# Probabilities of pairs six to 31 copied by DMA into fp32r tiles and transposed as fp32r; second-layer sums in place; the 1e-9 added by GpSimd

## Chip, core and metric

The kernel runs on one core of one Trainium2 chip. The metric is the device time in microseconds (us). The core has five engines with an instruction queue each: PE (TensorE, matmuls; PEld is its weight load), DVE (VectorE), ACT (ScalarE), POOL (GpSimd) and SP (SyncE, which here only issues DMAs). SBUF is the memory that engines compute from, PSUM the one that PE writes to.

## What is computed

Attention with a decay for 8 batches of 8 heads, 576 tokens, head dimension 64, and behind it a token mix and a two-layer channel network, all in float32:

```python
scores = scale * np.matmul(q, k.transpose(0, 1, 3, 2))
cum = np.cumsum(np.log(np.clip(f, 0.0001, 1.0)), axis=-1)
scores = np.where(causal, -1e9, scores + cum[..., :, None] - cum[..., None, :])
attn = np.exp(scores - np.max(scores, axis=-1, keepdims=True))
attn = attn / (np.sum(attn, axis=-1, keepdims=True) + 1e-09)
x = np.matmul(attn, v)                       # heads side by side: (8, 576, 512)
u = x + (x.transpose(0, 2, 1) @ U @ V).transpose(0, 2, 1)
out = u + np.maximum(u @ w_ch1, 0.0) @ w_ch2 # 512 -> 2048 -> 512
```

## The kernel before

**Pairs and slots.** Two heads make a pair; there are 32, four to a batch. A step handles one pair in ten slots, and works on three pairs at once: slots 0 to 3 score pair p for its first head (`score(p, 0, i)`, i the block of 128 queries), slots 4 and 5 the 64 last queries of both heads (`score_tail`), slots 6 to 9 the second head. In the same slots PE transposes the probabilities of the pair before (`turn_p`, `turn_tail`, `turn_small`), multiplies them with the values (`values`), and turns and ranks the results of the pair before that (`turn_x`, `ranks`). Parts of the token mix and of the first channel layers of the batch before fill the slots (`mix_units`, `ffn_units`). When the pairs are through, at about 740 us, the other ten of 16 hidden blocks follow for all batches.

**Two kinds of pair.** Pairs 0 to 5 (`p < NF`) multiply in plain fp32. From pair six on, operands are split into a high and a low fp32r tile and multiplied in fp32r. The probabilities of all pairs are written as F32 by the exponential and transposed as F32 with `ident`; what comes out is split behind the transpose, by a copy on ACT (`PTh`) and a subtraction on DVE (`PTl`).

**One score's way.** PE writes scores into a bank of PSUM (`S`, two of them from pair six on). In the next slot DVE adds the mask and takes the extreme value (`top`, L387), ACT writes the exponential and its row sum (`use`, L395), and so frees the bank. `inverse` adds the two sums of the tail (POOL, L435), adds 1e-9 (DVE, L436) and inverts (DVE, L437).

**What sets the order.** `defer(phase, fn, slots)` puts work into a later slot, by phase. PE's order is written out by hand for all steps, SP's for step 0 and from step 8 on. ACT, DVE and POOL, and SP in steps 1 to 7, are ordered by a scheduler when the program is built. Each queue runs in its order: an instruction that waits holds up all behind it. A tile from a pool with n buffers waits until the tile n allocations earlier is read.

**Buffers near the change.** `P0` to `P3` have two buffers each, `Ptl` (tail probabilities) and `cr` (a half of a product) one, `ost` (a sum of the second layer on its way to DRAM) two.

Of the kernel before, what the change touches and what calls it, by code (L numbers as in the profile page):

```python
# [44 lines left out]
def tile_decay_attention_moe(ctx, tc, qk, v, f, U, V, w1, w2, out):  # L45
# [43 lines left out]
    sf2 = pool("sf2")  # L89
# [6 lines left out]
    sb3 = pool("sb3", 3)  # L96
    psF = ctx.enter_context(tc.tile_pool(name="psF", bufs=2, space=PSUM))
# [30 lines left out]
    ident = cst.tile([P, P], F32, name="ident")  # L128
    make_identity(nc, ident)
# [14 lines left out]
    def decay_log():  # L144
        fr = sb.tile([B * H, S], F32, tag="xT", name="fr")
        fl = sb.tile([B * H, S], F32, tag="cr", name="fl")
        cm = sb.tile([B * H, 4, S], F32R, tag="PT", name="cm")
        return fr, fl, cm
# [48 lines left out]

    def load_w(u):
# [4 lines left out]
        if kind == "w2":  # L203

            spare = xn[NX - 1].rearrange("p c d -> p (c d)").bitcast(I32)
            if fc % 2:
                raw, a = spare[:, 1536:2560], sb.tile([P, 512], I32, tag="w2a", name=f"stg{u}")
            else:
                raw, a = spare[:, 0:1024], spare[:, 1024:1536]
# [167 lines left out]

    def score(p, j, i):
# [25 lines left out]
    def score_tail(p, x):  # L404
# [14 lines left out]
        def use():  # L419
            if x == 1:  # L420
                z["ptl"] = sb.tile([P, S], F32, tag="Ptl", name=f"Ptl{p}")
                for y in range(2):
                    nc.scalar.activation(
                        z["ptl"][:, hw * y : hw * y + hw], z["tl"][y][:, :hw], AF.Exp, bias=z["nm"][:, 9:10],
                        scale=-1.0, accum_out=z["sm"][:, 8 + y : 9 + y],
                    )

# [3 lines left out]
    def inverse(p):  # L431
# [4 lines left out]
        nc.vector.tensor_scalar(sm[:, 0:9], sm[:, 0:9], 1e-9, None, op0=ALU.add)  # L436
# [12 lines left out]
    def turn_p(p, j, g):  # L449
# [16 lines left out]
        for x, (c, i) in enumerate(grp):  # L466
            nc.tensor.transpose(tp[:, P * x : P * x + P], z["P"][j][i][:, P * c : P * c + P], ident)  # L467
# [12 lines left out]
    def turn_tail(p):  # L480
        z = st[p]
        tp = z["tv"][:, 512:1024]
        for c in range(NM):
            nc.tensor.transpose(tp[:, P * c : P * c + P], z["ptl"][:, P * c : P * c + P], ident)
# [13 lines left out]
    def turn_small(pa, px):  # L498

        tq = psT.tile([P, 512], F32, tag="T", name=f"Ty{pa}_{px}")  # L500
        if pa is not None:
            nc.tensor.transpose(tq[0:64, 0:P], st[pa]["ptl"][:, MAIN:S], ident)
# [75 lines left out]
    def values(p, j):  # L578
# [4 lines left out]
        if j == 0:  # L583
            z["xT"] = sb.tile([P, S], F32, tag="xT", name=f"xT{p}")
            z["cr"] = sb.tile([P, S], F32, tag="cr", name=f"cr{p}")
        VS, xT, cr = z["VS"], z["xT"], z["cr"]
# [14 lines left out]
        def total():  # L601
            nc.vector.tensor_tensor(xT[OWN[j]], pv[OWN[j], X0 : X0 + S], cr[OTH[j]], op=ALU.add)
# [3 lines left out]
        defer(1, lambda: nc.scalar.copy(cr[OTH[j]], pv[OTH[j], X0 : X0 + S]))  # L606
# [66 lines left out]
    def mix_units(b):  # L673
# [38 lines left out]
        def tv():  # L712
# [9 lines left out]
            def use():  # L722
                for x, t in enumerate((uh, ul)):
                    if b < B - 1:
                        nc.sync.dma_start(ud[b, :, x], t.bitcast(F32)[:, :, 0:MAIN])
                    if b % 2:
                        jt = b // 2
                        nc.sync.dma_start(ud[B, :, x, :, P * jt : P * jt + P], t.bitcast(F32)[:, :, MAIN : MAIN + P])

            defer(4, use, 2)  # L730
# [5 lines left out]
    def ffn_units(b):  # L736
# [7 lines left out]
        for t0, nt in groups:  # L744
# [24 lines left out]
            def l2(x, part, t0=t0, g=g):  # L769
# [17 lines left out]
                def use():  # L787
                    if b == B - 1 and ci < NM:
                        nc.vector.tensor_tensor(X[:, ci], ps, X[:, ci], op=ALU.add)
                        return  # L790
                    ost = sf2.tile([P, DM], F32, tag="ost", name=f"ost{b}_{ci}")
                    if ci < NM:
                        nc.vector.tensor_tensor(ost, ps, X[:, ci], op=ALU.add)
                        nc.sync.dma_start(accd[b, ci], ost)
                    else:
                        nc.vector.tensor_tensor(ost[0:64], ps[0:64], X[0:64, NM], op=ALU.add)
                        nc.vector.tensor_tensor(ost[64:128], ps[64:128], xn[(b - 1) % NX][0:64, NM], op=ALU.add)
# [876 lines left out]
```

## Time and profile before

| what | value |
|---|---|
| median of three runs | 1217.29 us (1216.34 to 1217.51) |
| the profiled execution, its own time | 1216.95 us |
| its span, first to last instruction | 1215.1 us |
| granted TensorE clock, mean | 0.999 |
| busy share of the span | PE 98%, DVE 76%, ACT 64%, POOL 28% |
| busy from 94.9 to 642.2 us (25 steps) | PE 537.3, DVE 400.6, ACT 400.6, POOL 272.5 us of 547.3 |

How it is read: a line of groups names kernel line, engine, operation, output tile and input tiles, shape, how many, then busy us, mean ns of one, and idle time before them with what ended it. A timeline gives start and duration in us; instructions that follow one another are merged as x4, and their duration then runs from the first start to the last end. A matmul's duration holds its way through the array, which the next one overlaps, so the pace of PE is read from the distance of starts. "Pair 14" below is the one whose step begins at 269.8 us.

### The profile page before, as it was taken

To read this page: it belongs to the slowest core of one execution; us is meant where nothing else is said; L and a number is where in the kernel's file an instruction comes from. 1 tells how busy PE (TensorE), PEld (TensorE's weight loads), DVE (VectorE), ACT (ScalarE), POOL (GpSimd) and SP (SyncE) were. 2 spreads that over 40 slices of the span, in tenths; PEclk is the share of its full clock that TensorE was granted. 3 is DMA by queue.
4 is the path that set the end of the run, shared out by engine and by line. 5 is a ranking of instruction groups with operands and counts; after the bars stand their busy time and mean duration, and the time that the engine had idled before them with its cause. 6 is when DMAs were issued, how large, how long until landed. Compare 5 with 4: busy or idle time off the path is not lost.

```text
span 1215.1 us, 24243 instructions
## 1 busy us (share of the span) xinstructions
PE 1190.5 (98%) x8463; PEld 1101.9 (91%) x8463; DVE 917.9 (76%) x2302; ACT 779.0 (64%) x2045; POOL 335.9 (28%) x366
## 2 busy tenths in 40 slices
PE   8999999999999999999999999999999999999997
PEld 6888888998999988999988898888999999999997
DVE  8786778668777677767769899848868778687765
ACT  7787777767777667777667444335565565555553
POOL 3656654444545535555442100000000000000000
PEclk9999999999999999999999999999999999999999
DMA  6546235225244334335324566936765574654643
GB/s 201 154 135 177 63 90 179 77 80 169 70 109 150 89 95 136 98 82 166 101 69 143 186 213 235 332 134 225 255 216 184 170 235 149 233 194 154 200 114 105
DMA packets 111243, 187.38 MB, mean 154 GB/s; under 512 B 11241, under 2 KB 55529, under 8 KB 109073
## 3 DMA queue, kind: packets, MB, share of 16 engines
q1 hardware_dynamic: 110848, 185.57, 49.2%
q8 instruction: 67, 1.10, 0.4%
q14 instruction: 56, 0.45, 0.1%
q10 hardware_dynamic: 272, 0.26, 0.1%
HBM read 137.42 MB, written 48.37 MB: 153 GB/s over the span
## 4 chain that ended last, share of the span: by engine, by line
PE 84%; DVE 6%; ACT 5%; issue 1%; DMA 1%; POOL 1%; POOLq 0%; ACTq 0%; DVEq 0%
PE pf L1312 16%; PE B L779 11%; PE A L758 10%; PE po L1404 8%; PE V L591 4%; PE px L1404 4%; PE T L467 3%; PE S L366 3%; PE S L367 2%; PE Hb L1135 2%; PE O L1151 2%; PE pf L1404 2%; PE po L1419 2%; ACT G L320 2%; PE V L548 1%
## 5 line engine op out<-in xcount | busy, mean ns | idle before, releaser
L1535 ACT COPY mc<-pf 128x512 f32<-128x512 f32 x139 | 81.6, 587 | 169.0 <-PE pf L1312 169.0
L387 DVE CUSTOM_DVE_ANT_0 S<-S,mask 128x128 f32<-128x128 f32 (+3 forms) x256 | 125.2, 497 | 56.3 <-PE S L367 48.1
L395 ACT ACTIVATE P<-S,nm 128x128 f32<-128x128 f32 (+3 forms) x256 | 136.3, 534 | 44.6 <-DVE nm L387 43.7
L1463 POOL TENSOR_TENSOR xn<-xn,xn 128x512 f32<-128x512 f32 x1 | 1.3, 1267 | 530.0 <-DMA out_dram<-xn 530.0
L758 PE MATMUL A<-uh,w1h 128*128 128x256 f32 (+1 forms) x384 | 119.7, 312 | 0.0
L758 PE MATMUL A<-ul,w1h 128*128 128x256 f32 (+1 forms) x384 | 113.5, 295 | 0.0
L758 PE MATMUL A<-uh,w1l 128*128 128x256 f32 (+1 forms) x384 | 113.5, 295 | 0.0
L320 POOL CAST G<-qk 64x576 fp32r<-64x576 f32 x52 | 34.4, 661 | 243.1 <-PE St L367 155.2
L779 PE MATMUL B<-w2h,hh 128*128 128x512 f32 x216 | 88.4, 409 | 0.0
L467 PE MATMUL T<-ident,P 128*128 128x128 f32 x544 | 86.8, 275 | 0.0
L779 PE MATMUL B<-w2l,hh 128*128 128x512 f32 x216 | 85.1, 394 | 0.0
L779 PE MATMUL B<-w2h,hl 128*128 128x512 f32 x216 | 84.7, 392 | 0.0
L445 DVE TENSOR_TENSOR PT<-T,PT 128x512 fp32r<-128x512 f32 (+1 forms) x156 | 79.0, 530 | 6.5 <-ACT PT L442 4.7
L591 PE MATMUL V<-PT,VS 128*128 128x448 f32 (+2 forms) x416 | 79.5, 333 | 0.0
L336 POOL TENSOR_TENSOR G<-qk,G 64x576 fp32r<-64x576 f32 x52 | 74.5, 1433 | 7.3 <-ACT G L320 5.6
L442 ACT CAST PT<-T 128x512 fp32r<-128x512 f32 (+1 forms) x156 | 67.7, 466 | 13.8 <-PE T L467 11.7
L366 PE MATMUL S<-G 128*128 128x128 f32 x208 | 71.7, 348 | 4.8 <-ACT P L395 2.3
L335 POOL TENSOR_TENSOR G<-qk,G 64x576 fp32r<-64x576 f32 x52 | 74.6, 1434 | 3.8
L758 PEld LDWEIGHTS A<-uh,w1l 128*128 128x128 f32 x384 | 73.1, 190 | 0.3
L758 PEld LDWEIGHTS A<-uh,w1h 128*128 128x128 f32 x384 | 72.8, 190 | 0.4
L758 PEld LDWEIGHTS A<-ul,w1h 128*128 128x128 f32 x384 | 72.8, 190 | 0.0
L591 PEld LDWEIGHTS V<-PT,VS 128*128 128x128 f32 x416 | 68.2, 189 | 3.0
(278 smaller groups left out, 3941.0 us busy)
## 6 DMA issues: line engine op xcount, KB each, us to landing
qk<-in_qk_dram SPq DMA_DIRECT2D x104, 288.0 KB
un<-ud SPq DMA_DIRECT2D x16, 1024.0 KB
d<-ud SPq DMA_DIRECT2D x48, 256.0 KB
twd<-xn SPq DMA_DIRECT2D x40, 256.0 KB
Th<-twd SPq DMA_DIRECT2D x35, 256.0 KB
tw<-twd SPq DMA_DIRECT2D x35, 256.0 KB
Tl<-twd SPq DMA_DIRECT2D x35, 256.0 KB
vr<-in_v_dram SPq DMA_DIRECT2D x32, 256.0 KB
```

The costliest lines, as they stand in the source:

```text
L335: el.tensor_tensor(g[oth, 2, cols], k[oth], gf[oth, 2, cols], op=ALU.subtract)
L366: nc.tensor.matmul(ps, G[j][:, 0, c0 : c0 + P], G[j][:, 2, cols], start=first, stop=False)
L387: nc.vector.tensor_tensor_reduce(ps[:, :w], ps[:, :w], mask[:, 512 - w : 512], scale=-SCALE, scalar=3.0e38, op0=ALU.add, op1=ALU.min, accu ...
L395: nc.scalar.activation(pt, ps[:, :w], AF.Exp, bias=z["nm"][:, col : col + 1], scale=-1.0, accum_out=z["sm"][:, col : col + 1])
L445: defer(2, lambda: nc.vector.tensor_tensor(dstl, src, dsth.bitcast(F32), op=ALU.subtract))
L467: nc.tensor.transpose(tp[:, P * x : P * x + P], z["P"][j][i][:, P * c : P * c + P], ident)
L591: nc.tensor.matmul(pv[:, X0 + lo : X0 + S], VS[:, c, j], pt[:, j, OC[c] + lo - P * c : OC[c] + S - P * c], start=x == 0 and c == 0, stop=F ...
L758: nc.tensor.matmul(ps[:, :nt], wt[:, fc, c], ut[:, c, sl], start=m == 0, stop=m == 3 * NDC - 1)
L779: nc.tensor.matmul(ps, ht[:, fc, P * x : P * x + P], wt[:, fc], start=fc == 0 and m == 0 and t0 // P + x == NM, stop=fc == NA - 1 and m == 2,)
L1312: nc.tensor.matmul(ps, a[x][:, c], b[y][:, c], start=start and m == 0, stop=m == 5, skip_group_check=True)
L1404: nc.tensor.matmul(ps[:, HT * x : HT * x + HT], f[a][:, P * x : P * x + P], w[b], start=k.i == 0 and m == 0 and x == 0 and not (k.n == NG ...
L1535: nc.scalar.copy(mc, FA)
```

## The change

From pair six on, the exponential writes a staging tile `E` (or `Et` for the tail) instead of `P`; one slot later SP issues a DMA that copies the staging tile into `P` (or `Ptl`), now declared fp32r. The DMA moves the words as they are. `flip` transposes these tiles with `identr`, an fp32r tile of the identity, into the same PSUM tile seen as fp32r; `ident` is the same tile seen as F32. All staging tiles come from one pool `sb4` with three buffers under one tag; `cr` and the scratch of the odd `w2` blocks come from it too. In `inverse`, POOL adds the 1e-9. The second layer's sums go back to the batch's tile `X` in place of `ost`, and the DMA that stores them follows two slots later. The store of `u` goes out in pieces of one block of 128 columns, one a slot. `place_decay(p + 1, 0)` is issued in slot 6, not 7. At the start POOL makes the identity in a scratch tile and casts it to `identr`, behind two memsets of `xn`. At the end of the pairs, one unit of the weight work is held a turn longer. The core of the diff:

```diff
+    sb4 = pool("sb4", 3)
-    ident = cst.tile([P, P], F32, name="ident")
-    make_identity(nc, ident)
+    identr = cst.tile([P, P], F32R, name="ident")
+    ident = identr.bitcast(F32)
+    unit = sb.tile([P, P], F32, tag="xl", name="unit")
+    make_identity(nc, unit)
+    nc.gpsimd.tensor_copy(identr, unit)
...
+    def stage(name):
+        return sb4.tile([P, S], F32, tag="stg", name=name)
+
+    def flip(p, dst, src):
+        if p < NF:
+            nc.tensor.transpose(dst, src, ident)
+        else:
+            nc.tensor.transpose(dst.bitcast(F32R), src, identr)
...
-            pt = sb2.tile([P, w], F32, tag=f"P{i}", name=f"P{p}_{j}{i}")
+            pt = sb2.tile([P, w], F32 if p < NF else F32R, tag=f"P{i}", name=f"P{p}_{j}{i}")
             z["P"][j].append(pt)
+            e = pt if p < NF else stage(f"E{p}_{j}{i}")
             nc.scalar.activation(
-                pt, ps[:, :w], AF.Exp, bias=z["nm"][:, col : col + 1], scale=-1.0, accum_out=z["sm"][:, col : col + 1]
+                e[:, :w], ps[:, :w], AF.Exp, bias=z["nm"][:, col : col + 1], scale=-1.0,
+                accum_out=z["sm"][:, col : col + 1],
             )
+            if p >= NF:
+                defer(6, lambda: nc.sync.dma_start(pt.bitcast(F32), e[:, :w]))
...
+                if p >= NF:
+                    defer(6, lambda: nc.sync.dma_start(z["ptl"].bitcast(F32), e))
...
-        nc.vector.tensor_scalar(sm[:, 0:9], sm[:, 0:9], 1e-9, None, op0=ALU.add)
+        nc.gpsimd.tensor_scalar(sm[:, 0:9], sm[:, 0:9], 1e-9, None, op0=ALU.add)
...
-            nc.tensor.transpose(tp[:, P * x : P * x + P], z["P"][j][i][:, P * c : P * c + P], ident)
+            flip(p, tp[:, P * x : P * x + P], z["P"][j][i][:, P * c : P * c + P])
...
-        defer(1, lambda: nc.scalar.copy(cr[OTH[j]], pv[OTH[j], X0 : X0 + S]))
+        def cross():
+            z["cr"] = stage(f"cr{p}_{j}")
+            nc.scalar.copy(z["cr"][OTH[j]], pv[OTH[j], X0 : X0 + S])
+
+        defer(1, cross)
...
+            pieces = [(x, c) for x in range(2) for c in range(NDC + 1) if (b < B - 1 if c < NDC else b % 2)]
+            for k, piece in enumerate(pieces):
+                defer(4, lambda piece=piece: store(*piece), 2 + k)
...
+                def store():
+                    if ci >= NM:
+                        for r, src in enumerate((X, xn[(b - 1) % NX])):
+                            nc.sync.dma_start(accd[B, b // 2, 64 * r : 64 * r + 64], src[0:64, NM])
+                    elif b < B - 1:
+                        nc.sync.dma_start(accd[b, ci], X[:, ci])
 
                 defer(1, use)
+                defer(6, store, 2)
...
             if s == 6 and NF <= nxt_p < NP:
+                place_decay(p + 1, 0)
                 at(5, lambda: parts(p + 1, 0, ENGINES))
```

PE's instructions stand in the same order as before. Three other places:

SP, in pair 14 from its slot 6 on (`qk` loads of pair 15 and 16, `G` the decay rows, `P` and `Ptl` the copies). Before:

```order
L282 DMA qk_1_3671<-in_qk_dram 64x1152 x2
L794 DMA accd<-ost_3_3691 128x512
L341 DMA G_91<-cumd 4x2x576
L341 DMA G_92<-cumd 4x2x576
L282 DMA qk_0_3790<-in_qk_dram 64x1152 x2
```

and now:

```order
L347 DMA G_91<-cumd 4x2x576
L288 DMA qk_1_3839<-in_qk_dram 64x1152 x2
L445 DMA Ptl_3827<-Et_3828 128x576
L824 DMA accd<-xn_115 128x512
L413 DMA P_10_3861<-E_10_3862 128x128
L413 DMA P_11_3897<-E_11_3898 128x256
L347 DMA G_92<-cumd 4x2x576
L413 DMA P_12_3930<-E_12_3931 128x384
L288 DMA qk_0_3964<-in_qk_dram 64x1152 x2
L747 DMA ud<-uh_3704 128x512
L413 DMA P_13_3954<-E_13_3955 128x512
```

The copies stand between the loads, each behind a wait for its exponential; the copy of `E_13` stands right behind a `qk` load.

ACT, in pair 14 from the tail's exponential to the second head's first two (`cr` copies half of a product of `values`). Before:

```order
L423 ACTIVATE Ptl_3660,sm_3485<-St_1_3639,nm_3484 128x288
L690 CAST uh_3546<-Tu_2_3648 128x4x128
L442 CAST PT_3512<-T_10_3674 128x512
L442 CAST PT_3512<-T_11_3701 128x384
L395 ACTIVATE P_10_3695,sm_3485<-S_10_3685,nm_3484 128x128
L395 ACTIVATE P_11_3730,sm_3485<-S_11_3698,nm_3484 128x256
L606 COPY cr_3706<-V_0_3707 64x576
```

and now:

```order
L440 ACTIVATE Et_3828,sm_3640<-St_1_3805,nm_3639 128x288
L712 CAST uh_3704<-Tu_2_3814 128x4x128
L461 CAST PT_3669<-T_10_3842 128x512
L461 CAST PT_3669<-T_11_3868 128x384
L408 ACTIVATE E_10_3862,sm_3640<-S_10_3853,nm_3639 128x128
L626 COPY cr_0_3895<-V_0_3873 64x576
L408 ACTIVATE E_11_3898,sm_3640<-S_11_3865,nm_3639 128x256
```

`E_11`, which takes over the buffer of `Et`, stands behind the copy to `cr` now.

DVE, where pair 14 ends and pair 15 begins (`sm` the row sums, `rv` their inverse, `xT` the product's two halves added). Before:

```order
L387 ISA S_00_3793,nm_3778<-S_00_3793,mask 128x128
L387 ISA nm_3778 128x1
L691 TENSOR_TENSOR ul_3547<-Tv_3773,uh_3546 128x4x64
L436 TENSOR_SCALAR sm_3485<-sm_3485 128x9
L437 RECIPROCAL rv_4072<-sm_3485 128x9
L387 ISA S_01_3825,nm_3778<-S_01_3825,mask 128x256
L387 ISA nm_3778 128x1
L602 TENSOR_TENSOR xT_3705<-V_1_3796,cr_3706 64x576
L604 TENSOR_TENSOR xT_3705<-V_1_3796,xT_3705 64x128
```

and now:

```order
L713 TENSOR_TENSOR ul_3705<-Tv_3945,uh_3704 128x4x64
L399 ISA S_01_4001,nm_3950<-S_01_4001,mask 128x256
L399 ISA nm_3950 128x1
L620 TENSOR_TENSOR xT_3872<-V_1_3970,cr_1_3991 64x576
L622 TENSOR_TENSOR xT_3872<-V_1_3970,xT_3872 64x128
L464 TENSOR_TENSOR PT_3981<-T_00_3983,PT_3981 128x512
L399 ISA S_02_4032,nm_3950<-S_02_4032,mask 128x384
L399 ISA nm_3950 128x1
L464 TENSOR_TENSOR PT_3981<-T_01_4004,PT_3981 128x384
L456 RECIPROCAL rv_4268<-sm_3640 128x9
```

The addition has left DVE, and the inversion stands behind four more of its operations.

## Rows read from the trace of the kernel before

**Rows 1.** The page: busy time by engine with the share of the span, and the chain that ended last by engine.

```profile
PE 1190.5 (98%) x8463; PEld 1101.9 (91%) x8463; DVE 917.9 (76%) x2302; ACT 779.0 (64%) x2045; POOL 335.9 (28%) x366
...
PE 84%; DVE 6%; ACT 5%; issue 1%; DMA 1%; POOL 1%; POOLq 0%; ACTq 0%; DVEq 0%
```

**Rows 2.** Busy us of each engine in three stretches: 25 steps of pairs 6 to 31, their end, and the rest; then granted clock, share of the DMA engines, GB/s.

```profile
94.90:642.20 547.30, 537.33 (x3738) 494.94 (x3738) 400.55 (x1134) 400.60 (x1127) 272.48 (x279) 1.00 0.39 111
642.20:740.00 97.80, 94.23 (x624) 85.94 (x623) 89.39 (x203) 54.60 (x131) 11.25 (x13) 1.00 0.55 190
740.00:1215.10 475.10, 468.44 (x3551) 449.36 (x3549) 351.80 (x755) 248.99 (x579) 1.27 (x1) 1.00 0.59 196
```

**Rows 3.** Groups of PE's transposes of probabilities in the whole span, shapes apart: 20 (T and T_v of L467), 4 and 1 for each of 32 pairs; seven of the last stand under another name.

```profile
L467 PE MATMUL T<-ident,P 128*128 128x128 f32 x544 | 86.8, 275 | 0.0
L484 PE MATMUL T_v<-ident,Ptl 128*128 128x128 f32 x128 | 19.2, 272 | 0.0
L467 PE MATMUL T_v<-ident,P 128*128 128x128 f32 x96 | 16.0, 275 | 5.1 <-DVE xT L604 5.0
L502 PE MATMUL Ty<-ident,Ptl 128*64 128x128 f32 x25 | 6.8, 272 | 0.0
```

**Rows 4.** PE's timeline, five places in order of what they show: four F32 transposes; fp32r matmuls of the same 128 columns with 64 columns of weights; four F32 transposes of 64 columns; four fp32r matmuls of 128 columns with 128 columns of weights, and the one behind them.

```profile
303.23 0.60 PE L484 MATMUL T_v<-ident,Ptl 128*128 128x128 f32 x4
...
309.44 0.22 PE L651 MATMUL Tt<-xh,Us 128*64 128x128 f32 x1
309.49 0.22 PE L651 MATMUL Tt<-xl,Us 128*64 128x128 f32 x1
309.55 0.22 PE L651 MATMUL Tt<-xh,Us 128*64 128x128 f32 x1
...
103.44 0.43 PE L717 MATMUL Tv<-ident,xn 64*128 64x64 f32 x4 [0.19 <-DVE ul L691]
...
98.40 0.64 PE L706 MATMUL Tu<-VV,TS 128*128 128x128 f32 x4
98.88 0.34 PE L366 MATMUL S<-G 128*128 128x256 f32 x1
```

**Rows 5.** The durations (minimum, median, maximum ns) of the transposes of 64 columns.

```profile
L717 PE MATMUL Tv<-ident,xn x32: 221/223/272, 103.4 to 712.0; 64*128 64x64 f32 x32
```

**Rows 6.** PE's timeline in pair 14, from the last tail score to the first scores of the second head.

```profile
281.64 0.30 PE L367 MATMUL St<-G 128*128 128x288 f32 x1
281.78 0.60 PE L484 MATMUL T_v<-ident,Ptl 128*128 128x128 f32 x4
...
283.04 0.62 PE L467 MATMUL T<-ident,P 128*128 128x128 f32 x4
...
284.89 0.22 PE L366 MATMUL S<-G 128*128 128x128 f32 x1
```

**Rows 7.** ACT's timeline in the same stretch and on to the second score of pair 15.

```profile
281.71 0.73 ACT L634 CAST xh<-xn 128x640 fp32r<-128x640 f32 x1 [1.40 <-DVE xn L520]
...
284.90 0.21 ACT L423 ACTIVATION_READ_ACCUMULATOR Ptl<-St,nm 128x1 f32 x1
...
287.56 0.64 ACT L606 COPY cr<-V 64x576 f32<-64x576 f32 x1 [0.23 <-PE V L597]
...
292.77 0.20 ACT L395 ACTIVATION_READ_ACCUMULATOR P<-S,nm 128x1 f32 x1
...
295.20 0.48 ACT L395 ACTIVATE P<-S,nm 128x256 f32<-128x256 f32 x1
295.57 0.21 ACT L395 ACTIVATION_READ_ACCUMULATOR P<-S,nm 128x1 f32 x1
```

**Rows 8.** PE's timeline: the score that takes over the bank which the exponential at 295.20 reads.

```profile
298.18 0.39 PE L366 MATMUL S<-G 128*128 128x512 f32 x1
```

**Rows 9.** A store of 256 KB out of SBUF on SP's queue, and the ACT instruction that waited for it to land.

```profile
761.08 0.32 SPq L1064 DMA_DIRECT2D twd<-xn  x1
...
764.31 0.41 ACT L182 CAST xn<-xn 128x256 fp32r<-128x256 f32 x1 [3.24 <-DMA twd<-xn]
```

**Rows 10.** The addition of 1e-9: its durations (minimum, median, maximum ns) over all pairs, its group, then DVE, POOL and PE around the one of pair 14.

```profile
L436 DVE TENSOR_SCALAR sm<-sm x32: 160/344/1421, 20.7 to 668.2; 128x9 f32<-128x9 f32 x32
...
L436 DVE TENSOR_SCALAR sm<-sm 128x9 f32<-128x9 f32 x32 | 18.0, 564 | 8.3 <-ACT P L395 7.3 <-POOL G L336 1.0
...
293.08 1.42 DVE L436 TENSOR_SCALAR sm<-sm 128x9 f32<-128x9 f32 x1 [0.33 <-ACT P L395]
...
293.03 1.43 POOL L335 TENSOR_TENSOR G<-qk,G 64x576 fp32r<-64x576 f32 x1
...
295.95 0.29 DVE L604 TENSOR_TENSOR xT<-V,xT 64x128 f32<-64x128 f32 x1
...
296.39 0.52 PE L467 MATMUL T_v<-ident,P 128*128 128x128 f32 x3 [0.76 <-DVE xT L604]
```

**Rows 11.** The start: POOL's identity and the memsets behind it, and ACT's first use of the identity.

```profile
1.22 0.29 POOL masks.py:199 TENSOR_SCALAR_AFFINE_SELECT ident<-ident 128x128 f32<-128x128 f32 x1
1.57 0.98 POOL L845 MEMSET xn<- 64x512 f32 x2
...
2.27 2.10 ACT L299 ACTIVATE qk<-G,ident 32x576 f32<-32x576 f32 x3
4.43 0.68 ACT L834 ACTIVATE fl<-fr 64x576 f32<-64x576 f32 x1
```

More of the change, by code (lines that the diff above doesn't have):

```diff
@@ L145, in decay_log @@
         fr = sb.tile([B * H, S], F32, tag="xT", name="fr")
-        fl = sb.tile([B * H, S], F32, tag="cr", name="fl")
+        fl = sb.tile([B * H, S], F32, tag="Ptl", name="fl")
         cm = sb.tile([B * H, 4, S], F32R, tag="PT", name="cm")
@@ L584, in values @@
             z["xT"] = sb.tile([P, S], F32, tag="xT", name=f"xT{p}")
-            z["cr"] = sb.tile([P, S], F32, tag="cr", name=f"cr{p}")
-        VS, xT, cr = z["VS"], z["xT"], z["cr"]
+        VS, xT = z["VS"], z["xT"]
         pv = psV.tile([P, 1024], F32, tag="V", name=f"V{p}_{j}")
@@ L720, in tv, with store @@
             evac_u(uh[:, :, to : to + TAIL], ul[:, :, to : to + TAIL], tv_)
[L722 to L730, printed above, removed]
+            def store(x, c):
+                t = (uh, ul)[x].bitcast(F32)
+                if c < NDC:
+                    nc.sync.dma_start(ud[b, :, x, c], t[:, c, 0:MAIN])
+                else:
+                    jt = b // 2
+                    nc.sync.dma_start(ud[B, :, x, :, P * jt : P * jt + P], t[:, :, MAIN : MAIN + P])
+            pieces = [(x, c) for x in range(2) for c in range(NDC + 1) if (b < B - 1 if c < NDC else b % 2)]
+            for k, piece in enumerate(pieces):
+                defer(4, lambda piece=piece: store(*piece), 2 + k)
         t = [(0.68, lambda i=i: tu(i)) for i in range(NM)]
@@ L787, in use @@
                 def use():
-                    if b == B - 1 and ci < NM:
+                    if ci < NM:
                         nc.vector.tensor_tensor(X[:, ci], ps, X[:, ci], op=ALU.add)
                         return
[L791 to L797, printed above, removed]
-                        nc.sync.dma_start(accd[B, b // 2], ost)
+                    for r, src in enumerate((X, xn[(b - 1) % NX])):
+                        rows, own = slice(64 * r, 64 * r + 64), src[0:64, NM]
+                        nc.vector.tensor_tensor(own, ps[rows], own, op=ALU.add)
+                def store():
+                    if ci >= NM:
+                        for r, src in enumerate((X, xn[(b - 1) % NX])):
+                            nc.sync.dma_start(accd[B, b // 2, 64 * r : 64 * r + 64], src[0:64, NM])
+                    elif b < B - 1:
+                        nc.sync.dma_start(accd[b, ci], X[:, ci])
                 defer(1, use)
+                defer(6, store, 2)
             units += [(12 * max(nt / 2400, 0.107), lambda fc=fc, l1=l1: l1(fc)) for fc in range(NA)]
@@ L1078, in tile_decay_attention_moe @@
             held -= 1
-            if wb and (wb[0] != (2, 1) or held < 0):
+            if wb and (wb[0] != (2, 1) or held < -1):
                 if wb[0] == (2, 1):
@@ L1275, in tile_decay_attention_moe @@
     Tl = sf.tile([P, NM + 1, DM], F32R, tag="ul", name="Tl")
[L1276 removed]
+    MC += [up.tile([P, DM], F32, name="mc2"), sf.tile([P, DM], F32, tag="TS0", name="mc3")]
     slots.update({7: Th[:, NM], 4: Tl[:, NM]})
```

17 lines of the change are left out of this document (7 added, 10 removed).

## The prediction

> **What bounds the kernel now.** I read the page first: busy shares and the chain of work that ended last [rows 1]. PE is busy for 98% of the span and carries 84% of the chain, DVE and ACT 6% and 5%. Then the stretches [rows 2]: of 547.3 us in which pairs 6 to 31 are at work PE is busy for 537.3, ACT and DVE for 400.6 each. So PE's work is the first limit there, with the other two at 73%; they matter where PE waits for one of them at one place. The last stretch, 475 us, has no work that the change touches. The granted clock is 1.00 in the pairs' stretch, so time lies in the number and pace of PE's instructions and in its waits. Third, the transposes [rows 3]: 544 + 96 + 128 + 32, thus 25 for each of 32 pairs; 26 pairs change, 650 transposes.
>
> **The transposes, removed and added.** A duration of 272 ns is not what one costs, since they overlap. Four in a row last 0.60 us [rows 4], so starts lie (0.60 - 0.272) / 3 = 0.109 us apart. No row shows an fp32r transpose. Its bounds come from the nearest rows. Below: fp32r matmuls that stream the same 128 columns, with 64 columns of weights, start 0.06 us apart (309.44, 309.49, 309.55) [rows 4], about half of 0.109. With 128 columns of weights the load could be the limit: F32 transposes of 64 columns behind a full load start (0.43 - 0.223) / 3 = 0.069 us apart [rows 4, 5], so that load takes no more. Above: fp32r matmuls with 128 columns of weights, not transposes, take (98.88 - 98.40) / 4 = 0.12 us each [rows 4], which their load must explain, as half the load gives half the pace. I take 0.065, between 0.06 and 0.069, because the load of the F32 transposes is the nearest one to an fp32r transpose's: the same mode, the same 128 columns of four bytes. The saving is then 0.044 x 650 = 28.6 us of PE's time, with ends at 0.049 x 650 = 31.9 and, at 0.12, a loss of 0.011 x 650 = 7.2.
>
> A rule speaks against it. Rows 4 show 64 columns behind a full load at 0.069 us. The Trainium skill (page "TensorE: Matmul & The Clock Gate", section "LDWEIGHTS (loading the stationary operand)") gives the load of a stationary operand as its columns over 1.2 GHz, an estimate of 107 ns for 128. By that rule a transpose could not come under 107 ns whatever its type, and the term above would be near 0. The row at 0.069 disagrees with the rule for F32 transposes, the row at 0.12 agrees for fp32r matmuls; no run here shows which holds for fp32r transposes.
>
> **What of this PE can keep.** In pair 14 the last tail score starts at 281.64 and the next score at 284.89 [rows 6]; the next needs the bank that ACT's two tail exponentials free, and those end at 285.11 after a burst that begins at 281.71 [rows 7]. This stretch is ACT's, not PE's. The eight transposes in it [rows 6] would save 8 x 0.044 = 0.35 us, and PE would wait that long more. Taken for every pair that is 0.35 x 26 = 9.2 us given back; the end on the other side is 0, where ACT starts its burst as much earlier. Left: 28.6 - 9.2 = 19.4 us.
>
> **The copies and their staging tiles.** ACT does the same exponentials and copies as before, at the same cost. New are nine DMAs a pair, 234 in all, and 41.7 MB (two heads of 128 rows by 1280 words and a tail of 128 by 576, in 26 pairs). The stretch moves 111 GB/s x 547 us = 61 MB now [rows 2]; 103 MB would be 188 GB/s, and the last stretch moves 196 without PE suffering [rows 2]. SP issues one in 0.32 us [rows 9], 75 us of 547, free. A transposed tile is needed about ten slots after its exponential, so PE doesn't feel a copy's way. What can be felt is the staging tile: with three buffers, ACT waits until the copy of three tiles ago has read its tile. The price of a copy, from a 256 KB store: issued at 761.08, its waiter went on at 764.31, so 3.2 us with other transfers beside it [rows 9]; a shorter one is issued in 0.32 us at least. Two places are short. The tail's tile: written at 285.11, wanted again by the exponential that now stands behind the copy to `cr`, which ends at 288.20 [rows 7]; 3.1 us are there for 3.2. The last tile of the second head: written at 292.97, wanted at 295.20 [rows 7]; 2.2 us for 3.2, so ACT is held for 1.0 us. PE feels that only past the bank's slack: the exponential ends at 295.78, the score that needs its bank starts at 298.18 [rows 7, 8]. The slack of 2.4 us covers it in this pair. But ACT's later work is held too, so I charge 0.15 us a pair, 4 us; the ends are 0 and 1.0 x 26 = 26. Queued on SP behind a waiting copy are the `qk` loads and decay rows; they are wanted half a step later, so 0.
>
> **The 1e-9.** The addition takes 160 to 1421 ns, 18.0 us in all, and DVE waits 7.3 us for ACT before it [rows 10]. The long ones lie under a POOL operation: 293.08 to 294.50 beside POOL's 293.03 to 294.46. DVE's next two steps come late then, its `xT` ends at 296.24, and PE waits 0.76 us for that [rows 10]; all such waits are 5.0 us [rows 3]. Removed from DVE, it costs POOL a small operation at its end of the pair, where POOL is half idle [rows 2], and the inversion stands four DVE operations later, so DVE hardly waits for it. I take 4 us gained; ends 0 and, with what else stands behind it on DVE, 7.
>
> **The rest.** The cast at the start stands behind the `xn` memsets, which end at 2.55, so the identity comes at about 2.8 instead of 1.51, and ACT, which used it at 2.27 with the logarithm right behind its three operations [rows 11], starts 0.5 us later: +0.5, between 0 and 1. Sums in place write as many elements from DVE as before, and their stores are read only in the last stretch; pieces of the `u` store are short issues on SP; the held weight unit and the earlier decay rows lie under a PE that is 96% busy [rows 2]. These I cost at 0, between -1 and +1; without that cover a held unit would cost a few us once.
>
> **Sum.** -28.6 + 9.2 + 4 - 4 + 0.5 = -18.9 us, against the profiled execution of 1216.95 us, which is 0.3 under the median: 1198 us.
>
> **The rivals.**
>
> *Not faster as fp32r.* If the transpose takes two turns for its four bytes in either type, or a load holds it at the present 0.109, the first two terms vanish: +4 - 4 + 0.5, thus 1217 or 1218; with the ends of the small terms 1211 to 1224. For it: no row shows such a transpose, and the 0.109 is the pace of a transpose whose type is as wide. Against: fp32r matmuls stream the same 128 columns in 0.06, and the load of 128 columns is done in 0.069 [rows 4, 5]. The Trainium skill's rule on loads, above, would end here.
>
> *Held by an fp32r load.* At 0.12 PE has 7.2 us more, all on the path: 1216.95 + 7.2 + 0.5 = 1225. For it: the row at 0.12. Against: the load under the F32 transposes of 64 columns takes no more than 0.069 [rows 4, 5].
>
> *Slower, by the staging tiles.* The copy of the second head's last tile stands right behind two `qk` loads of 288 KB. At the 190 GB/s of the busier stretch [rows 2] these take 3.1 us; if the copy must come behind both, it lands 6.3 us after its exponential instead of 3.2, and ACT is held 6.3 - 2.2 = 4.1 us, 1.7 past the slack of 2.4. That is 1.7 x 26 = 44 us on PE in place of my 4: 1238. It decides from the point where the copy lands more than 2.2 + 2.4 + (18.9 + 4) / 26 = 5.5 us after its exponential. For it: one queue in order, two loads of that size in every pair. Against: SP issues the loads as soon as the copy ahead of them is out, before that exponential ends, so they have a start on the copy.
>
> *All of it kept.* ACT's burst moves with PE and no tile is late: -28.6 - 4 + 0.5, thus 1185.
>
> **How the numbers follow.** The forecast has 0.58, with a range of its own from 1187 to 1209; not faster as fp32r 0.22; the staging tiles 0.10; the load 0.06; all kept 0.04. About 0.2%, 2.4 us, is what a measurement of this kernel can tell from no change. Faster by more: 0.57 + 0.07 + 0.04 = 0.68. Within: 0.01 + 0.09 + 0.01 + 0.01 = 0.12. Slower by more: 0.06 + 0.09 + 0.05 = 0.20. The range of 1187 to 1224 leaves out most of all kept, most of the staging case and half of the load's, 0.15, and a little of the forecast.
>
> **What would show it.** In the changed profile: transposes of L467's kind starting 0.06 to 0.07 us apart (0.109 or 0.12 for the rivals); PE's busy time to about 642 us down by 20 to 28 us, its idle time up by some 8; waits of the second head's first score for the tail's exponential longer; ACT waiting for copies at the second score of a pair, about 1 us (4 for the staging case); no DVE operation of 1.4 us on nine columns, and no wait of PE for `xT`; the last stretch as before. The prediction is wrong if the transposes keep their pace, or if PE's waits grow by as much as they shrink.

## The result, and the profile after

The changed kernel takes 1224.47 us (median of 6 runs, 1220.87 to 1228.23) beside 1217.01 of the kernel before (6 runs, 1216.34 to 1217.51): a ratio of 1.006, with an interval of 1.0041 to 1.0079. It is slower by 0.6%, where 1198 was forecast and 1224 was the end of the range. The profiled execution took 1228.23 us, its span is 1226.4; it is the slowest of the six, in part because of the clock, as shown below.

The page of the changed kernel, busy time and the chain that ended last, beside [rows 1]:

```profile
PE 1187.0 (97%) x8463; PEld 1092.1 (89%) x8463; DVE 899.8 (73%) x2270; ACT 774.3 (63%) x2045; POOL 346.5 (28%) x399
...
PE 68%; DMA 8%; ACT 5%; DVE 4%; issue 2%; SPq 0%; POOLq 0%; POOL 0%; ACTq 0%; DVEq 0%
```

PE is busy for 3.5 us less although the kernel is longer, and DMA, 1% of the chain before, is 8%. So the chain now runs through transfers that somebody waits for.

The windows of three stretches: 25 steps from the first score of pair 6, the end of the pairs, the rest (columns as in [rows 2]):

```profile
93.95:648.78 554.83, 534.17 (x3738) 486.69 (x3739) 388.07 (x1110) 397.74 (x1129) 280.17 (x304) 0.99 0.62 181
648.78:759.60 110.82, 103.38 (x661) 92.61 (x662) 95.46 (x217) 55.33 (x133) 12.50 (x14) 1.00 0.58 197
759.60:1226.40 466.80, 459.74 (x3511) 441.66 (x3509) 342.29 (x737) 246.70 (x576) 1.26 (x1) 1.00 0.60 196
```

The second stretch is cut here at the first `Hb`, the first matmul of the weight work behind the pairs. In the kernel before it was:

```profile
642.23:749.00 106.77, 103.20 (x662) 93.39 (x662) 98.28 (x219) 56.42 (x134) 11.22 (x13) 1.00 0.54 184
```

The same 25 steps took 547.3 us before [rows 2] with PE busy for 537.3, thus idle for 10.0; now they take 7.5 us more and PE is idle for 20.7. Behind the pairs another 4 us were lost. The DMA engines move 181 GB/s in the pairs, where 188 was forecast from the bytes; their busy share rose from 0.39 to 0.62.

The transposes by group, beside [rows 3]; 26 pairs are the changed ones:

```profile
L388 PE MATMUL T<-ident,P 128*128 128x128 f32 x442 | 55.4, 242 | 0.0
L388 PE MATMUL T_v<-ident,Ptl 128*128 128x128 f32 x104 | 11.9, 237 | 0.0
L388 PE MATMUL T_v<-ident,P 128*128 128x128 f32 x78 | 10.3, 242 | 1.6 <-DVE xT L622 1.6
...
L408 ACT ACTIVATE E<-S,nm 128x256 f32<-128x256 f32 x52 | 24.8, 476 | 24.5 <-DMA Ptl<-Et 19.0 <-DMA P<-E 3.8 <-DVE nm L399 0.9
```

The transposes are shorter (242 ns for 275) and PE's wait for `xT` fell from 5.0 to 1.6 us, both in the forecast direction. The last row is ACT's: exponentials of 256 columns in the changed pairs, idle for 24.5 us before them, 19.0 of it for the copy of the tail's tile. The view of waits sums all shapes (us in total, times, longest). The last line is of the kernel before, where ACT's exponentials write `P`:

```profile
PEld S L372 <- ACT E L408: 19.4, 25, 2.2
ACT E L408 <- DMA Ptl<-Et: 19.0, 14, 2.3
...
ACT E L408 <- DMA P<-E: 17.5, 19, 2.0
...
PE S L372 <- ACT E L408: 11.8, 20, 2.0
...
ACT xn L66 <- DMA xn<-in_w_dram: 8.4, 4, 3.2
```

```profile
PE S L366 <- ACT P L395: 2.3, 5, 0.7
```

PE's waits for exponentials ahead of a score thus rose from 2.3 to 11.8 us.

One such wait, row by row: the chain, and the timeline of SP's queue, ACT and PE.

```profile
307.68 4.94 DMA Ptl<-Et
```

```profile
305.47 1.14 SPq L288 DMA_DIRECT2D qk<-in_qk_dram  x2
306.66 0.58 SPq L747 DMA_DIRECT2D ud<-ul  x1
307.68 0.52 SPq L445 DMA_DIRECT2D Ptl<-Et  x1
...
309.77 0.64 ACT L626 COPY cr<-V 64x576 f32<-64x576 f32 x1 [0.91 <-ACT PT L461]
312.73 0.47 ACT L408 ACTIVATE E<-S,nm 128x256 f32<-128x256 f32 x1 [2.32 <-DMA Ptl<-Et]
...
313.35 0.50 PE L372 MATMUL S<-G 128*128 128x512 f32 x1 [0.98 <-ACT E L408]
```

Two `qk` loads of 288 KB go out at 305.47, a piece of the `u` store of 256 KB behind them, and the copy of the tail 2.2 us after the first load. It is in the chain for 4.94 us. ACT finished `cr` at 310.41 and waits 2.32 us for the staging tile, and the score that needs the bank of this exponential waits 0.98 us on PE.

PE's longest wait for a score stands at another place, the third score of a pair's first head, which takes the bank of that head's first exponential:

```profile
335.42 0.49 SPq L413 DMA_DIRECT2D P<-E  x1
335.96 1.25 SPq L288 DMA_DIRECT2D qk<-in_qk_dram  x2
...
341.30 0.37 ACT L408 ACTIVATE E<-S,nm 128x128 f32<-128x128 f32 x1 [1.67 <-DMA P<-E]
...
341.81 0.44 PE L372 MATMUL S<-G 128*128 128x384 f32 x1 [1.99 <-ACT E L408]
```

In the program as built this exponential takes the tile of the second head's third one, whose copy went out at 335.42, ahead of the loads. A DMA raises its semaphore 16 times, once for each part; in this trace 15 parts of that copy had landed 2.2 us after the issue and the last one after 5.8. The other long wait at this place (1.44 us at 229.50) looks the same: 15 parts after 2.3 us, the last after 4.9, just ahead of the exponential.

The clock, in windows ahead of, in and behind a dip at 165 us, and one at 342.5:

```profile
155.00:165.00 10.00, 7.44 (x56) 6.66 (x55) 6.40 (x20) 7.34 (x22) 5.35 (x6) 1.00 0.50 135
165.00:168.40 3.40, 3.40 (x16) 3.10 (x16) 1.57 (x6) 1.48 (x5) 0.15 (x1) 0.50 0.45 145
168.40:178.00 9.60, 9.60 (x78) 9.18 (x78) 6.08 (x21) 7.06 (x20) 5.45 (x6) 1.00 0.56 148
336.00:342.50 6.50, 4.51 (x37) 4.21 (x35) 3.40 (x11) 4.74 (x13) 4.65 (x4) 1.00 0.66 166
```

For 3.4 us the granted clock is 0.50, 1.2 of 2.4 GHz. In the 10 us ahead PE was idle for 2.56, in the 6.5 ahead of the second dip for 1.99. There are three dips in this execution, at 165.0, 342.5 and 383.4 us, each worth about 1.7 us (an estimate, half of its length), and none before the last microseconds in the kernel before. The last long waits ahead of them are 1.43 us for `xT`, the 1.99 us above, and 0.61 and 0.89 us for an exponential and for DVE; so not every one is a wait for a copy. Of the six runs those with a mean clock of 0.998 took 1221 and 1222 us and this one, at 0.994, took 1228.

### The profile page after: what moved, and what is told of

Same layout as the page of the kernel before. It is cut to its first block, busy times and chain, and to the rows that moved or that the text cites. A ratio compares the mean times of both kernels' runs of the same rounds, so it can differ in the third digit from the quotient of the medians.

```text
span 1226.4 us, 25010 instructions
## 1 busy us (share of the span) xinstructions
PE 1187.0 (97%) x8463; PEld 1092.1 (89%) x8463; DVE 899.8 (73%) x2270; ACT 774.3 (63%) x2045; POOL 346.5 (28%) x399
## 4 chain that ended last, share of the span: by engine, by line
PE 68%; DMA 8%; ACT 5%; DVE 4%; issue 2%; SPq 0%; POOLq 0%; POOL 0%; ACTq 0%; DVEq 0%
PE pf L1338 16%; PE B L803 8%; PE po L1430 8%; PE A L782 7%; PE px L1430 4%; PE V L609 3%; DMA Ptl<-Et 3%; PE S L372 3%; PE O L1177 2%; PE po L1445 2%; PE pf L1430 2%; PE Hb L1161 2%; PE S L373 2%; DMA P<-E 2%; PE T L388 2%
## 5 line engine op out<-in xcount | busy, mean ns | idle before, releaser
L408 ACT ACTIVATE E<-S,nm 128x128 f32<-128x128 f32 x208 | 110.6, 532 | 68.3 <-DMA Ptl<-Et 19.0
L464 DVE TENSOR_TENSOR PT<-T,PT 128x512 fp32r<-128x512 f32 (+1 forms) x156 | 78.5, 526 | 19.4 <-ACT PT L461 18.6
L372 PE MATMUL S<-G 128*128 128x128 f32 x208 | 74.0, 359 | 19.2 <-ACT E L408 11.8
L326 ACT CAST G<-qk 128x576 fp32r<-128x576 f32 x104 | 64.7, 672 | 9.3 <-issue 9.0
```

The lines of the kernel that those rows point to most:

```text
L326: i = eng.copy(dst, src) if eng is nc.scalar else eng.tensor_copy(dst, src)
L372: nc.tensor.matmul(ps, G[j][:, 0, c0 : c0 + P], G[j][:, 2, cols], start=first, stop=False)
L408: nc.scalar.activation(e[:, :w], ps[:, :w], AF.Exp, bias=z["nm"][:, col : col + 1], scale=-1.0, accum_out=z["sm"][:, col : col + 1],)
L464: defer(2, lambda: nc.vector.tensor_tensor(dstl, src, dsth.bitcast(F32), op=ALU.subtract))
```

## Experiments

The theory: PE has less to do, but ACT is held for staging tiles whose copies land late, and PE waits for ACT; the gain is given back there. Against it: another engine would hold PE as soon as its work shrinks; or the copies cost by their traffic, whatever the number of tiles.

**Five staging tiles.** Room for them comes from a bf16 mask.

```
-    mask = att.tile([P, ZR + HW], F32, name="mask")
+    mask = att.tile([P, ZR + HW], mybir.dt.bfloat16, name="mask")
-    def stage(name):
+    def stage(name, w=S):
+        if w <= 2 * P:
+            return sb.tile([P, w], F32, tag=f"stg{w}", name=name)
```

> Five staging tiles in place of three: the exponentials of 128 and of 256 columns get a tile each of their own, so a tile of the other three is written again over 6 us after its last use; room comes from a bf16 mask. If the three tiles are what gave the gain back, ACT's waits for P<-E and Ptl<-Et (36.5 us in the changed kernel) fall under 5 us, PE's waits for the exponentials by some 13 us, the granted clock has no dips in the pairs, and the time is 1205 to 1213. If the next engine would have held PE anyway, the waits move to another releaser and the time stays at 1221 to 1226. If it is the copies' traffic that delays the loads of qk and of the weights, the staging waits vanish but the time falls by less than 5 us.

Measured: 1210.91 us, ratio 0.9943 (0.9928 to 0.9958). No wait of ACT for a copy is left in the pairs, and 13.6 us of the 1224.5 are gone. One dip of the clock is left, at 130 us. The control has the mask alone:

> The changed kernel with a bf16 mask and its three staging tiles, the control for five tiles. If the mask's type does nothing by itself, 1223 to 1227. If it is what made five tiles faster (DVE reads half the bytes of one operand), DVE's masked minima are shorter than before and the time is 1210 to 1216.

1224.16 us, 1.0057 (1.004 to 1.0073): the mask by itself changes nothing that can be told from noise.

**No copies at all.**

```
-            e = pt if p < NF else stage(f"E{p}_{j}{i}")
+            e = pt
-            if p >= NF:
-                defer(6, lambda: nc.sync.dma_start(pt.bitcast(F32), e[:, :w]))
```

and the same for the tail.

> The exponentials write the fp32r tiles themselves, with no copies and no staging; left out is the exact copy, so the probabilities are rounded. If copies and staging gave the gain back, the transposes still start 0.065 us apart and the time is 1196 to 1206, below five staging tiles by the 4 us that the changed kernel lost after the last pair. If the next engine holds PE anyway, 1215 or more.

1204.66 us, 0.9898 (0.988 to 0.9915). So copies and staging cost 19.8 us in the changed kernel. Its first two stretches:

```profile
93.95:629.73 535.78, 525.64 (x3739) 482.27 (x3739) 386.95 (x1110) 400.48 (x1129) 279.85 (x304) 1.00 0.40 113
629.73:736.30 106.57, 102.24 (x662) 92.74 (x662) 95.37 (x217) 55.75 (x134) 12.00 (x14) 1.00 0.57 187
```

Between the two profiled executions 19.1 us lie in the 25 steps, where PE's idle time falls from 20.7 to 10.1 and the dips of the clock are gone, and 4.3 behind them.

**F32 transposes**, on the copied tiles, with three tiles and with five, and on tiles without copies. The edit is `nc.tensor.transpose(dst, src.bitcast(F32), ident)` for the pairs from six on.

> Copies and staging as in the changed kernel, the transposes as F32 on the same tiles. If the transposes gain what their pace says, PE has 28 us more work here; ACT then has more time in each pair, so its waits for copies fall by half or so, and the time is 1232 to 1245. If the transposes' pace was worth nothing because another engine holds PE, it stays at 1222 to 1228.

> The changed kernel without copies and with F32 tiles and F32 transposes: what is left of the change beside copies and fp32r. From the starts in the traces of the fp32r kernels, 60 to 87 ns apart within a run and 84 to 86 ns from the last of a run to the next instruction (28 behind an F32 one), I now give a run of four 0.06 us and a pair about 0.4 us, 10 us in all. Then this kernel is at 1213 to 1217, 8 to 12 above the same with fp32r tiles (1204.7). If the transposes gain 0.044 us each as predicted, less the 9 us that ACT's burst keeps, it is at 1222 to 1226, and the rest of the change costs 5 us or more.

> Five staging tiles, the transposes as F32. If a copy costs only through its staging tile, this is within 2 us of the kernel without copies and with F32 transposes. If the copies' traffic costs by itself, it is 4 to 7 us above that one, as five tiles stand to no copies with fp32r (1210.9 to 1204.7).

With three tiles, without copies, with five tiles: 1227.45 us, 1.0079 (1.0064 to 1.0094); 1213.69 us, 0.997 (0.9957 to 0.9982); 1227.39 us, 1.0085 (1.007 to 1.01). Thus fp32r is worth 9.0 us without copies, 3.0 in the changed kernel, 16.5 with five tiles. In the changed kernel the pace is worth little, as expected for the case that another engine holds PE. The third was a miss: it should have stood within 2 us, or 4 to 7, of the kernel without copies, and stands 13.7 above it. Its waits name as much of the reason as can be seen, 6.7 us where the kernel without copies has 0.2:

```profile
PE T_v L390 <- DVE xT L624: 6.7, 13, 2.4
```

No copy is waited for by ACT there; PE waits for `xT`. Where one of these waits falls (583 us), DVE's addition to `xT` stands behind a masked minimum and an evacuation; DVE and ACT get their order from a scheduler, and other tiles gave it another one. The other 7 us are not explained. So the five tiles tell what the waits cost only together with a changed order.

Why fp32r is worth 9 us and not 19: the tail's run of four transposes and the first instruction behind it, without copies, with F32 and then with fp32r tiles.

```profile
300.80 0.60 PE L388 MATMUL T_v<-ident,Ptl 128*128 128x128 f32 x4
301.15 0.36 PE L778 MATMUL A<-uh,w1h 128*128 128x256 f32 x1
```

```profile
298.55 0.45 PE L388 MATMUL T_v<-ident,Ptl 128*128 128x128 f32 x4
298.84 0.35 PE L778 MATMUL A<-uh,w1h 128*128 128x256 f32 x1
```

The next instruction starts 0.35 us after the run's first transpose with F32, 0.29 with fp32r: 0.06 us for four, where 0.176 was forecast. Single starts, over 25 pairs of the two kernels: F32 transposes follow each other after 109 ns, and the instruction behind the last one after 28; fp32r ones after 61, 65 and 84 ns (medians), and the instruction behind the last after 84 to 86. In the runs of four of `P` alone the first step is longer, 134 with F32 and 102 with fp32r.

**One line: 1e-9 on GpSimd**, in the kernel before.

```
-        nc.vector.tensor_scalar(sm[:, 0:9], sm[:, 0:9], 1e-9, None, op0=ALU.add)
+        nc.gpsimd.tensor_scalar(sm[:, 0:9], sm[:, 0:9], 1e-9, None, op0=ALU.add)
```

> The kernel before with one line changed: 1e-9 added by GpSimd. Predicted gain 4 us, ends 0 and 7: 1210 to 1217. If DVE's late xT was covered by PE's other waits, 1216 to 1218.

1210.12 us, 0.9945 (0.993 to 0.996): 6.7 us for one line, at the upper end. Its group, and PE's wait for `xT`, 5.0 us before [rows 3]:

```profile
L436 POOL TENSOR_SCALAR sm<-sm 128x9 f32<-128x9 f32 x32 | 8.2, 258 | 16.4 <-ACT P L395 14.0
```

```profile
PE T_v L467 <- DVE xT L604: 0.2, 1, 0.2
```

**Where the copy is issued.** First on ACT's queue (`nc.scalar.dma_start` in both places).

> The copies are issued from ACT's queue instead of SP's, so none stands behind a qk load in the queue, and none waits on SP. If the place behind the loads is what makes a copy late, ACT's waits for copies fall under 15 us and the time is 1208 to 1218, less what nine issues a pair cost ACT. If the transfer engines themselves are shared in order, a copy still lands 4 to 6 us after its exponential, the waits stay over 25 us, and the time is 1224 or more.

1252.14 us, 1.0289 (1.0243 to 1.0335). The waits stayed, so SP's queue alone is not what makes a copy late. What the other 28 us are is not settled: ACT's row order changed in many places, and PE's clock dipped seven times in the profiled execution (mean 0.985).

```profile
ACT E L408 <- DMA P<-E: 20.7, 15, 2.5
...
ACT E L408 <- DMA Ptl<-Et: 16.5, 14, 2.1
```

Then the `qk` loads were moved in SP's order, from slots 0 and 6 of a step to 3 and 5, and to 3 and 4.

```
-            if s == 0 and ps_ and p:
+            if ps_ and p and s == (0 if p < NF else 3):
                 load_qk(p + 1, 0)
-            if s == 6 and ps_:
+            if ps_ and s == (6 if p < NF else 5):
```

> The changed kernel, its copies and three staging tiles, with the qk loads of pairs from seven on issued in slots 3 and 5 instead of 0 and 6, so that they run ahead of the copies with the longest time to spare. If copies are late because their packets run behind those of the qk loads, ACT's waits for copies fall from 36 us to under 20 and the time to 1209 to 1218. If a copy is late by its own transfer or by the other traffic, the waits stay over 30 and the time within 3 us of 1224.

> The changed kernel with the qk loads issued in slots 3 and 4: further from the tail's copy, which moving them to 3 and 5 left behind the second load, and a slot further from the casts that read the second one. If a copy is late because load packets run ahead of it, both kinds of waits of ACT for copies are under 10 us in all; and if these waits are what PE lost the gain to, the time is 1208 to 1216. If the waits go and the time stays at 1221 or more, PE's loss stands elsewhere (the order on DVE and ACT).

1227.88 us, 1.009 (1.0062 to 1.0119), and 1228.14 us, 1.009 (1.0067 to 1.0113). Waits of the pairs' stretch, for slots 3 and 5 and then for 3 and 4:

```profile
ACT E L408 <- DMA Ptl<-Et: 21.6, 17, 2.1
...
ACT G L326 <- DMA qk<-in_qk_dram: 9.9, 8, 2.3
...
ACT E L408 <- DMA P<-E: 2.2, 6, 1.0
```

```profile
PEld S L372 <- ACT Et L440: 13.5, 27, 1.7
...
ACT cr L626 <- DMA P<-E: 11.3, 7, 2.1
ACT E L408 <- DMA Ptl<-Et: 11.0, 14, 2.0
...
ACT E L408 <- DMA P<-E: 3.9, 8, 1.1
```

In the first the waits for `P<-E` fell from 17.5 to 2.2 us: slot 0, ahead of the copies of the second head's last tiles, has no load now. `Ptl<-Et`, still right behind a load, kept its waits. In the second those fell to 11.0. So a load ahead makes a copy late, though not every late copy has one, as the copy issued at 335.42 shows, which went out ahead of the loads. But other waits came in their place, of ACT's casts for `qk`, of `cr` for a copy, of PE for the tail's exponentials, and the time did not move. Neither reached the expected time, and the sum of ACT's waits was not what set it.

**The tail without its copy**, the eight copies of P a pair as they are.

```
-                e = z["ptl"] if p < NF else stage(f"Et{p}")
+                e = z["ptl"]
```

with its copy taken out.

> The changed kernel with the tail's exponentials written straight to their fp32r tile (these are rounded), so that one copy and one staging tile a pair fall away; the eight copies of P stay. The waits for Ptl<-Et (19.0 us) end, but their tile's place in the round goes to another: if the waits are what costs, the time falls by about half of the 19.8 us between the changed kernel and the one without copies, to 1212 to 1217; if every copy costs by its traffic, by a ninth of it, to 1221 to 1223.

1206.55 us, 0.9923 (0.9906 to 0.994): 17.9 of the 19.8 us for one copy of nine, more than either theory gave. The rows say where. Waits of the pairs' stretch, the exponentials of 384 and 256 columns, and the windows of the first two stretches:

```profile
ACT E L408 <- DMA P<-E: 30.6, 28, 2.2
...
PE S L372 <- ACT E L408: 4.3, 14, 0.5
```

```profile
L408 ACT ACTIVATE E<-S,nm 128x384 f32<-128x384 f32 x52 | 30.4, 585 | 32.6 <-DMA P<-E 25.4 <-DVE nm L399 3.7 <-DVE PT L462 1.3
L408 ACT ACTIVATE E<-S,nm 128x256 f32<-128x256 f32 x52 | 24.8, 477 | 4.7 <-DMA P<-E 2.8 <-DVE PT L462 0.8 <-ACT PTh L459 0.5
```

```profile
94.02:632.68 538.66, 526.64 (x3738) 482.26 (x3738) 387.41 (x1110) 397.65 (x1129) 280.29 (x304) 1.00 0.59 173
632.68:738.20 105.52, 102.29 (x661) 92.83 (x662) 96.09 (x218) 55.13 (x132) 12.49 (x14) 1.00 0.60 205
```

ACT still waits 30.6 us for copies, in 28 places, and PE hardly notices. The waits have moved from the exponentials of 256 columns to those of 384. Counted by place in the timelines of pairs 6 to 31: before the second head's second exponential ACT is idle 20.1 us in the changed kernel and 0.5 here; PE, before the second head's last score, which takes the bank of that exponential, 5.4 us (9 times) and 0.3. PE's idle time before the first head's third score fell from 4.0 to 1.2, as without copies. Before the first head's third exponential ACT's idle time is 14.1 and 20.5 us, and PE's before the tail's scores, which take its bank, 1.9 and 2.4; before the second head's third 1.4 and 11.9, and PE's before the next pair's first score 5.7 and 2.6, where it is 2.6 without any copies. In all 22.6 us lie between the two profiled executions: 16.2 in the 25 steps (8.6 of PE's idle time, and the three dips, about 5), 5.3 behind them and 1.2 in the last stretch. The DMA share is 0.59 and the time 1.9 above that without any copy, so traffic is not what costs. Here too ACT and DVE have another order in places, so the split within the 17.9 is not exact.

**The rest of the change**, each in the kernel before with 1e-9 on GpSimd: the sums in place with their later stores (the `use` and `store` of the change), and the `u` store in pieces with the held unit (`held < -1`).

> The kernel before with 1e-9 on GpSimd and the second layer's sums in place, stored from xn a slot later. Predicted cost 0, which gives 1210; if the later stores hold xn, so that the weight rows load late after the last pair, 1212.5 to 1215, with longer waits of ACT for xn<-in_w_dram.

> The kernel before with 1e-9 on GpSimd, the u store in pieces a slot apart, and the held weight unit a slot later. Predicted cost 0, which gives 1210; if the pieces or the held unit delay the weights after the last pair, 1212.5 to 1215.

1212.98 us, 0.9962 (0.9947 to 0.9977), and 1211.23 us, 0.9951 (0.9936 to 0.9967), which is 2.9 and 1.1 over 1210.12; the 1.1 is not clear of noise, since the runs overlap (1210.29 to 1212.70 beside 1209.79 to 1211.25). In the first the held unit stays as before, so that the weight sums overwrite sums of the layer that are not yet stored; its time is that of the same work. ACT's waits for `xn<-in_w_dram` from 645 to 765 us are 4.6 us, 2.7 without the stores.

**The parts that gain, alone.** In the kernel before: 1e-9 on GpSimd, the exponentials of pairs six on straight to fp32r tiles, fp32r transposes; `cr`, sums and stores as before.

```
+            pt = sb2.tile([P, w], F32 if p < NF else F32R, tag=f"P{i}", name=f"P{p}_{j}{i}")
```

> The kernel before with 1e-9 added by GpSimd and with the exponentials of pairs six on written straight to fp32r tiles and transposed as fp32r; no copies, and cr, sums, stores, held unit and decay rows as before. The probabilities are rounded to fp32r here. If the gains add, 1210.1 less the 9.0 of the fp32r transposes: 1200 to 1203. If the 3.6 us that the rest of the change costs belong to the fp32r tiles or the cast at the start, 1204 to 1206.

1202.07 us, 0.9876 (0.9859 to 0.9894), as expected if the gains add: it beats both kernels, but with probabilities rounded to fp32r. Its first two stretches, and its chain:

```profile
93.98:629.27 535.29, 525.08 (x3739) 482.25 (x3739) 386.93 (x1110) 399.75 (x1129) 279.93 (x304) 1.00 0.40 113
629.27:733.50 104.23, 101.93 (x661) 92.63 (x662) 95.42 (x215) 55.63 (x132) 11.66 (x14) 1.00 0.54 187
```

```profile
PE 86%; DVE 5%; ACT 4%; issue 2%; DMA 1%; POOL 1%; POOLq 0%; ACTq 0%; DVEq 0%
```

Against the changed kernel's rows the pairs are 19.5 us shorter, the end 6.6, and DMA is 1% of the chain.

## Why the prediction was wrong, step by step

The medians make a ladder from one kernel to the other: 1217.0, 1210.1 with the line on GpSimd, 1202.1 with fp32r tiles, 1204.7 with the rest of the change, 1224.5 with the copies. Against the forecast the copies are 15.8 us too many and the transposes gain 11.4 too little; the 1e-9 gains 2.9 more and the rest costs 2.1 more, which makes the 26.4 us between 1198 and 1224.5. With either of the two large errors alone the kernel would still have been faster, at some 1214 or 1210.

- **The copies and their staging tiles: the step that failed.** Charged 4 us, they cost 19.8. One place was named, the tail's tile: "3.1 us are there for 3.2". The price was wrong. 3.2 us was read from one store in the last stretch [rows 9]; the tail's copy is issued behind the two loads of slot 6 and takes 4.94 us in the row above. I had put exactly this lateness, as a rival with 0.10, on the other short place, the second head's last tile, and there only. What came is slower, as in that rival, but at another place and by less. The wait for the tail's tile reached PE, which lost 5.4 us at the second head's last score; I had priced it at 0.1 us a pair, and all of ACT's waits together at 0.15 us a pair.
- **The round of tiles: read wrong.** That a tile waits for the one n allocations earlier does not hold strictly. In the program as built the second exponential of a first head mostly takes the tile of `cr`. The second head's last tile goes to the third exponential of the next pair in 21 of 26 pairs, not to the second, and there the slack did cover the waits: with the tail direct ACT's idle time of 20.5 us at this place is 2.4 on PE. The tile of the second head's third exponential goes to the next pair's first exponential in 24 pairs. This place was not in my sum, and PE's idle time behind it is 4.0 us, 1.2 without copies.
- **The granted clock.** I had it at 1.00 throughout. Three dips cost some 5 us in the profiled execution, which is the slowest. What brings them is not shown; waits behind a copy stand ahead of the second and the third, and the kernels without the tail's copy or without any have none in these 25 steps.
- **The transposes: right in kind, mis-sized.** -28.6 and +9.2 were forecast, -19.4 together; 8.1 to 9.0 were measured without copies. "0.065" holds between the first transposes of a run; the third and what stands behind the last came at 84 ns, and the 28 ns behind an F32 run were not in my sum. From start to next start the transposes of 25 pairs took 62.1 us before and 53.2 without copies, 8.9 less, where 0.044 x 625 gives 27.5. My method, the spacing inside a run, left out its last member. The rule that I weighed against the trace (the Trainium skill, "TensorE: Matmul & The Clock Gate", "LDWEIGHTS (loading the stationary operand)", an estimate of 107 ns for 128 columns) isn't what holds them: steps of 61 to 102 ns are below it.
- **What ACT's burst keeps.** With no copies PE's idle time before the second head's first score, the place that I named, rose from 1.3 to 3.1 us in 26 pairs: 1.8 us of the 9.2. Before the first head's first, which I had not named, it rose from 0.1 to 2.6.
- **The 1e-9: right, a little small.** 4 forecast with 7 as the end, 6.7 to 6.9 measured: 1.1 of it ahead of pair 6, 4.3 in 25 pairs, 1.5 behind. DVE's addition of 1.42 us beside POOL's operation of 1.43 [rows 10] takes 258 ns on POOL. With this agrees what the Trainium skill says (page "SBUF — State Buffer", section "SBUF: two separate sides"): VectorE and GpSimd share a pair of SBUF ports, and an instruction that takes the pair holds it to its end while the other engine waits. The trace agrees in so far as the two operations end together, at 294.50 and 294.46 [rows 10]. No run here shows that this addition uses the pair, or separates the ports from another reason for that delay.
- **The rest: not nothing.** +0.5, between -1 and +2, was forecast; 2.6 came with fp32r tiles and 3.6 with F32 ones, and the two parts alone cost 2.9 and 1.1, the latter within noise. The cover I named, a busy PE, ends with the last pair: 2.3 of the 2.6 us lie behind it (106.57 us without copies beside 104.23 with the gaining parts alone); there ACT waits for weight rows, and stores of the sums are in their way.

Of the expected signs, those of the transposes' starts (60 to 70 ns) came for the first two gaps only. PE's busy time in the 25 steps fell by 3.2 us, not by 20 to 28, and its idle time rose by 10.7 where some 8 were expected. DVE has no operation of 1.4 us on nine columns any more, as said (its inversion takes 0.2); one long wait for `xT`, of 1.43 us, is left. "ACT waiting for copies at the second score of a pair, about 1 us (4 for the staging case)" came at another place. PE's waits grew by more than they shrank, which is what the text named as proof against it.

Open stay the price of the changed order of DVE and ACT in the kernels with other tiles, the 4.3 us that the copies cost behind the pairs, why the last of a copy's 16 parts is sometimes late, and the cause of the longer time with the copies on ACT's queue.

## What to carry to other kernels

A new buffer in a rotation has as many deadlines as users. Read from the built program who takes which tile, price the copy at the place with the least slack, with the transfers that are queued ahead of it there, and don't take it from a quiet stretch. A sum of waits says little: 30.6 us of ACT's for copies cost 2 us at one place, and 36.5 cost 20 when some of them stood at others. Measure the pace of a run from its first start to the start of what follows it, and try the change without its most expensive helper, here the copy, before accepting the price.

## What was not expected of the hardware

- fp32r transposes of 128 columns start 61, 65 and then 84 ns apart in most runs, and hold the next instruction for 84 to 86; F32 ones 109, and 28.
- Three times, behind waits of 0.9 to 2.0 us, PE ran at 1.2 GHz for 3.4 us, in a stretch where it is over 95% busy on the whole.
- A copy within SBUF of 288 KB, issued 2.2 us after the first of two loads of the same size, stood in the chain for 4.94 us, and issuing the copies on another engine's queue left ACT's waits at 37 us. Another copy, issued ahead of the loads, had 15 of its 16 parts after 2.2 us and the last after 5.8.
- Nine columns on DVE took up to 1.42 us under a POOL operation, and one such instruction a pair cost the kernel 0.55%.
